# Windowed attention and a relu-squared expert: tokens brought in by casting and transposing transfers instead of by PE transposes

## The chip, the cores and the metric

The kernel runs on one core of one Trainium2 chip. The metric is the device time of one launch in microseconds (us), median of several runs. Each experiment was timed against runs of the kernel before on the same chip; a ratio is the mean time of one kernel's fast runs over that of the other's fast runs of the same rounds, so it is not quite the ratio of the medians. Chips differ: the kernel before took between 368.7 and 372.0 us (medians) on the chips used, so experiments are compared by ratio, and, where it can be done, by distances inside the traces, which mostly repeat from batch to batch to some hundredths of a us.

Engines: PE multiplies matrices (PEld loads its weights), ACT does activations, DVE elementwise work, POOL is GpSimd, SP only issues transfers. "Granted clock" is the share of PE's full clock that the records show; "half clock" is a stretch in which they show 0.5. In the kernel, SBUF is the on-chip memory that tiles live in, PSUM the one that matmuls write and other engines copy out of, and DRAM the memory off the core.

## The reference, cut to what matters

```python
# q, k, v: [8 batches, 8 heads, 576 tokens, 64]; 8 global tokens; window of 32 to each side
scores = scale * q @ k.T
mask   = (|i - j| <= 32) | is_global[i] | is_global[j]
attn   = softmax(where(mask, scores, -1e9)) @ v
x      = attn as [4608 tokens, 512]
out    = relu(x @ w_in)**2 @ w_out        # w_in [512, 2048], w_out [2048, 512]
```

Of the kernel before, what the change touches and what calls it, by code (L numbers as in the profile page):

```python
# [17 lines left out]
KT = 120  # L18
# [16 lines left out]
SCW = (456, 440)  # L35
MB = (0, 456)
NBUF = 5
# [3 lines left out]
def kernel(  # L41
# [33 lines left out]
    bufs_of = {"sc": 1, "acc": 1, "tr": 1, "mm": 3}  # L75

# [3 lines left out]
    st = {nm: sbt("st" + nm, [TP + NG, H, TJ, D], FP32) for nm in "kq"}  # L80
    st["v"] = sbt("stv", [P, NT, H, D], FP32)
    kts = [sbt(f"kt{i}", [P, NT, P], FP16) for i in range(NBUF)]
    qts = [sbt(f"qt{i}", [P, NCOL], FP16) for i in range(NBUF)]

    vts = [sbt(f"vt{i}", [P, NT, 3, D], FP16) for i in range(NBUF)]
    w_in = sbt("w_in", [P, NDM, dff], FP16)
    w_out = sbt("w_out", [P, NFF, dm], FP16)


    XOFF = 36  # L90
    xT = sbt("xT", [P, NDM, XOFF + B * S], FP16)

    nc.scalar.preload_act_table_set("natural_log_exp_and_others")


    g64 = sbt("g64", [1, NG], I64)
    src = {"k": k, "q": q, "v": v}
    gscr = {}

    def fetch_tokens(eng, nm, b, hp):  # L100
        hs = slice(2 * hp, 2 * hp + 2)
        eng.dma_start(
            out=st[nm][0:TP, hs].rearrange("p h j d -> p h (j d)"),
            in_=src[nm][b, hs].rearrange("h (p j) d -> p h (j d)", j=TJ),
        )

    def fetch_values(eng, b, hp):
        hs = slice(2 * hp, 2 * hp + 2)
        dst = st["v"]
        for h in range(2 * hp, 2 * hp + 2):  # L110
            eng.dma_start(
                out=dst[8 : 8 + KT, 0:4, h],
                in_=v[b, h, 0 : 4 * KT].rearrange("(t s) d -> s t d", s=KT),
            )
        eng.dma_start(
            out=dst[8 : 8 + KN[4], 4, hs], in_=v[b, hs, 4 * KT : S].rearrange("h s d -> s h d")
        )

    def fetch_globals(b, hp):
        def rows(nm):  # L120
            return gscr[(nm, b // 2)][b % 2, :, 2 * hp : 2 * hp + 2]


        for nm in "kq":
            js = range(TJ) if b == 2 else (TJ - 1,)
            for h in range(2):
                dst = st[nm][TP : TP + NG, 2 * hp + h, js[0] : TJ]
                nc.sync.dma_start(
                    out=dst, in_=rows(nm)[:, h].unsqueeze(1).to_broadcast((NG, len(js), D))
                )  # L130
        nc.sync.dma_start(
            out=st["v"][0:NG, :, 2 * hp : 2 * hp + 2].rearrange("p t h d -> p t (h d)"),
            in_=rows("v").rearrange("g h d -> g (h d)").unsqueeze(1).to_broadcast((NG, NT, 2 * D)),
        )

    fetch_tokens(nc.sync, "k", 0, 0)
    nc.scalar.dma_start(out=g64, in_=global_idx.unsqueeze(0))
    fetch_tokens(nc.scalar, "q", 0, 0)
    fetch_tokens(nc.scalar, "q", 0, 1)
    fetch_tokens(nc.sync, "k", 0, 1)  # L140
    fetch_values(nc.sync, 0, 0)
    fetch_values(nc.sync, 0, 1)
    fetch_tokens(nc.sync, "k", 0, 2)
    fetch_tokens(nc.sync, "q", 0, 2)
    fetch_values(nc.sync, 0, 2)
    fetch_tokens(nc.sync, "k", 0, 3)
    fetch_tokens(nc.sync, "q", 0, 3)
    fetch_values(nc.sync, 0, 3)


    idle = sbt("idle", [P, 512], FP16)
    nc.vector.memset(idle, 0.0)
    ones = sbt("ones", [1, P], FP16)
    nc.vector.memset(ones, 1.0)
    nc.scalar.copy(
        out=st["v"][0:NG].rearrange("p t h d -> p t (h d)"),
        in_=idle[0:NG].unsqueeze(1).to_broadcast((NG, NT, H * D)),
    )
# [52 lines left out]
    for kt in kts:  # L211
        nc.vector.memset(kt[:, 4, 8 + KN[4] : P], 0.0)

    def clear_values(op, vt):
        op(vt[:, :, 1], 1.0)
        op(vt[96:P, 4, 0:3:2], 0.0)

    for vt in vts[0:3]:
        clear_values(nc.gpsimd.memset, vt)


# [6 lines left out]

    gbf = sbt("gbf", [P, NG], FP32)
    g32, g32a, g32b = (sbt("g32" + x, [1, NG], I32) for x in ("", "a", "b"))  # L230
# [14 lines left out]
    def columns():  # L245
        nc.vector.tensor_scalar(out=g32a, in0=g32, scalar1=HS, scalar2=None, op0=ALU.min)
        nc.vector.tensor_scalar(
            out=g32b, in0=g32, scalar1=-255, scalar2=0, op0=ALU.add, op1=ALU.max
        )
# [15 lines left out]
    def mask_natural():  # L265
        for half in range(2):
# [17 lines left out]
    def mask_globals_matmul():  # L284


        mg = pst("acc", [P, 2, 512])
        for half in range(2):
            wins = [x for x in WIN[half] if x[3] > 8]
            for i, (t, so, c0, w) in enumerate(wins):  # L290
                o = c0 - half * BANKC
                nc.tensor.matmul(
                    mg[0:NG, half, o : o + w], oh[:, t, :],
                    mask[:, MB[half] + so : MB[half] + so + w],
                    start=(i == 0), stop=(i == len(wins) - 1), skip_group_check=True,
                )
        return mg

    far = sbt("far", [P, SCW[0] + SCW[1]], FP16)

    def mask_globals(mg, half):
        for t, so, c0, w in WIN[half]:
            for grp in range(4):
                lo, hi = max(grp * GRP, c0), min(grp * GRP + GTOK, c0 + w)
                lo, hi = max(lo, KT * t + 8 * grp), min(hi, KT * (t + 1) + 8 * grp)
                if lo < hi:
# [3 lines left out]
                        out=mask[0:NG, o : o + hi - lo], in_=mg[0:NG, half, a : a + hi - lo],  # L310
# [51 lines left out]
    def gather_rows(c):  # L362
        gsts = {nm: sbt("gst" + nm, [P, D], FP32) for nm in "kqv"}
        for nm, gst in gsts.items():
            nc.gpsimd.indirect_dma_start(
                out=gst, out_offset=None,
# [3 lines left out]
        return gsts  # L370

    def gather_store(c, gsts):
        for nm, gst in gsts.items():
            scr = dram.tile([P, D], FP32, name=f"gscr_{nm}{c}")
            nc.gpsimd.dma_start(out=scr, in_=gst)
            gscr[(nm, c)] = scr.rearrange("(b g h) d -> b g h d", b=2, h=H)



    nats = {}  # L380

    def cast_tokens(op, nm, i):
        b, hp = divmod(i, NHP)
        n = TP + NG if b > 1 else TP
        nat = nats[(nm, i)] = sbt("nat" + nm, [TP + NG, TJ, P], FP16, bufs=2)
        op(  # L386
            out=nat[0:n].rearrange("p j (h d) -> p h j d", d=D),
            in_=st[nm][0:n, 2 * hp : 2 * hp + 2],
        )

    def cast_values(op, i):
        hs = slice(2 * (i % NHP), 2 * (i % NHP) + 2)
        for tsl, n in ((slice(0, 4), P), (slice(4, 5), 8 + KN[4])):
            op(out=vts[i % NBUF][0:n, tsl, 0:3:2], in_=st["v"][0:n, tsl, hs])

    def v_globals(i):
        vs = vts[i % NBUF][:, :, 0:3:2]
# [4 lines left out]
        (nc.vector.tensor_copy if i == NHP - 1 else nc.scalar.copy)(out=gvs, in_=gl)  # L402
        nc.vector.tensor_copy(
# [4 lines left out]
    def transposed(nm, i):  # L408

        nat = nats.pop((nm, i))  # L410
        b = i // NHP
        tr = pst("mm" if b == 0 or (nm == "q" and i <= 2 * NHP) else "tr", [P, 1024], FP16)
        for j in range(TJ):
            n = TP + NG if (b > 1 and j == TJ - 1) else TP
            nc.tensor.transpose(  # L415
                tr[:, TP * j : TP * j + n], nat[0:n, j, :], identity[0:n, 0:n]
            )
        gl = tr[:, S : S + NG]
        if b < 2:
            gl = tr.bitcast(FP32)[:, 384 : 384 + NG]  # L420
            for j in range(TJ):
                nc.tensor.matmul(
                    gl, nat[0:TP, j, :], ohp[0:TP, j, :], start=(j == 0), stop=(j == TJ - 1),
                    skip_group_check=True,
                )
        return tr[:, 0:S].rearrange("p (j q) -> p q j", j=TJ), gl

    def tr_k(i, tail=None):
        tk, gl = transposed("k", i)
        kt = kts[i % NBUF]  # L430
        nc.vector.tensor_copy(
# [3 lines left out]
        (tail or nc.vector.tensor_copy)(  # L435
            out=kt[:, 4, 8 : 8 + KN[4]].rearrange("p (q j) -> p q j", j=TJ), in_=tk[:, 80:96]
        )
        nc.vector.tensor_copy(
            out=kt[:, :, 0:NG], in_=gl.unsqueeze(1).to_broadcast((P, NT, NG))
        )  # L440

    def tr_q(i, op=None):
        op = op or nc.vector.tensor_copy
        tq, gl = transposed("q", i)
        q4 = qts[i % NBUF].rearrange("p (g x) -> p g x", x=GRP)
# [5 lines left out]

# [62 lines left out]
    fills = []  # L514
    for half in range(2):
        for u in range(0, NFF, 2):
            fills.append((8 * half + 8, 2, mm1_half, (u, half)))
    for m in range(TC // P):
        for part in range(4):
            fills.append((16, 2, mm2, (0, m, part)))  # L520
    for c in range(1, NCH):
        n = (TC * (c + 1) + S - 1) // S
        ready = 16 * n + (0 if n == 2 else 4)
        for u in range(NFF):
            fills.append((ready, 2, mm1, (c, u)))
        for m in range(TC // P):
            for part in range(4):
                fills.append((ready, 2, mm2, (c, m, part)))

    def take(n):  # L530
        for _ in range(n):
            _, _, fn, a = fills.pop(0)
            fn(*a)

    credit = [0.0]

    def fill(step, n):
        credit[0] += n
        while fills and fills[0][0] <= step and credit[0] >= fills[0][1]:
# [335 lines left out]
```

## The kernel before: the parts that the change and the argument touch

Heads are handled in pairs, so a batch has four pairs; a pair is done in two halves of 288 tokens. The expert is cut into nine chunks of 512 tokens, and a chunk into 32 *units* of four matmuls with 512 columns: 16 units with the first matrix (`mm1`, each with a relu on ACT and a square on DVE) and 16 with the second (`mm2`). Units stand between the pieces of attention so that PE has work while ACT and DVE do the softmax.

```python
def cast_tokens(op, nm, i):              # f32 staging -> f16, on DVE (keys) or ACT (queries)
    ...
    op(out=nat[0:n].rearrange(...), in_=st[nm][0:n, 2 * hp : 2 * hp + 2])

def transposed(nm, i):                   # 6 PE transposes for one pair's keys or queries
    ...
    for j in range(TJ):
        nc.tensor.transpose(tr[:, TP * j : TP * j + n], nat[0:n, j, :], identity[0:n, 0:n])

def tr_k(i, tail=None):                  # three copies out of PSUM on DVE; tr_q has two more
    ...

def mm1(c, u):
    for t in range(NDM):
        nc.tensor.matmul(ph, w_in[:, t, u * P : (u + 1) * P], xT[:, t, ...], ...)
    nc.scalar.activation(out=rl, in_=ph, func=AF.Relu)
    nc.vector.tensor_tensor(out=gts[c][:, u, :], in0=rl, in1=rl, op=ALU.mult)

for i in range(2 * NHP, B * NHP):        # batches 2 to 7
    ...
    for half in range(2):
        et = scores(i, half)             # 10 matmuls in the first half, 6 in the second
        if i + 1 < B * NHP:
            (tr_k, tr_q)[half](i + 1)    # transposes for the next pair
        fill(2 * step, nf)               # two expert units
        if prev is not None:
            pv(*prev)                    # outputs of the half before
        fill(2 * step + 1, nf)           # two expert units
        casts(i + 2, half)               # casts for the pair after the next
```

After a batch's last pair, POOL writes the rows of the global tokens into `xT` (`scatter`). The first-matrix units of the chunk that follows need them.

The softmax here doesn't subtract the row's maximum and nothing guards it: scores larger than these inputs give would overflow.

## Time and profile before

| | before |
|---|---|
| time, median | 371.34 us |
| profiled span | 368.4 us |
| a steady batch (4 to 6) | 36.89 us |
| of this, 32 expert units | 27.7 us |
| first unit of chunk 1 starts | 84.19 us |
| expert work after the last attention | from 302.3 us to the end |

The page gives busy time and share of the span for each engine; the second group shows, in 40 equal slices, the busy tenths of PE, the granted PE clock and the share of the DMA engines.

```profile
PE 347.7 (94%) x2941; PEld 186.0 (51%) x2941; DVE 250.5 (68%) x656; ACT 249.2 (68%) x482; POOL 51.3 (14%) x143
PE   7779799988899999999999999999999989999995
...
PEclk9978999998999999999999999999999999999999
DMA  8999999787843663375336533652020011002002
```

Windows view, three stages: up to the first unit of chunk 1; batches 2 to 7; the rest. Columns: stretch, length, busy us of PE, PEld, DVE, ACT and POOL (instructions), granted clock, DMA share, GB/s.

```profile
0.00:84.20 84.20, 71.64 (x890) 46.55 (x891) 50.77 (x168) 50.52 (x97) 28.08 (x83) 0.96 0.95 191
84.20:302.40 218.20, 213.88 (x1765) 111.53 (x1765) 178.23 (x445) 178.37 (x350) 21.57 (x52) 0.99 0.43 114
302.40:368.00 65.60, 62.21 (x289) 27.97 (x286) 21.53 (x45) 20.36 (x35) 1.62 (x8) 1.00 0.12 45
```

PE timeline of one pair of batch 4: start, duration, what. Durations overlap: in the tail the record of a 512-column matmul lasts 379 ns, but the next one starts after 216.

```profile
153.55 0.40 PE L564 MATMUL sc<-qt_74,kt_69 64*128 64x160 f16 x10
153.88 0.43 PE L415 MATMUL tr<-identity,natk 96*128 96x96 f16 x6
154.16 1.89 PE L502 MATMUL mm<-w_out,gt 128*128 128x512 f16 x8
155.88 0.54 PE L602 MATMUL acc<-et,vt_78 128*128 128x112 f16 x6
156.26 1.89 PE L502 MATMUL mm<-w_out,gt 128*128 128x512 f16 x8
158.09 0.36 PE L564 MATMUL sc<-qt_74,kt_69 64*128 64x112 f16 x6
158.38 0.43 PE L415 MATMUL tr<-identity,natq 96*128 96x96 f16 x6
158.66 1.89 PE L502 MATMUL mm<-w_out,gt 128*128 128x512 f16 x8
160.38 0.63 PE L602 MATMUL acc<-et,vt_79 128*128 128x160 f16 x10
160.87 1.89 PE L502 MATMUL mm<-w_out,gt 128*128 128x512 f16 x8
162.69 0.39 PE L564 MATMUL sc<-qt_75,kt_70 64*128 64x160 f16 x10
```

The pair takes 162.69 - 153.55 = 9.14 us without a gap. Its eight units cost 6.92 us: in the tail the chain of waits shows 64 matmuls in 13.81 us, 0.216 us each, so 0.865 us a unit. That leaves 2.2 us of attention on PE.

### The profile page before, as it was taken

How to read it: one execution, taken by the hardware profiler on the slowest of the kernel's cores; microseconds unless marked ns; L12 is line 12 of the kernel's file. 1: busy time of each engine (PE TensorE's matmuls, PEld its weight loads, DVE VectorE, ACT ScalarE, POOL GpSimd, SP SyncE). 2: the span in 40 equal slices, each digit the busy share in tenths (PEclk: the TensorE clock that was granted, in tenths of full speed). 3: DMA queues.
4: the chain of work that ended last, by engine and by line, in shares of the span. 5: the costliest groups of instructions: out<-in, count | busy, mean ns of one | idle time of the engine just before them, and what ended most of it. 6: DMA issues, size and time to landing. Idle time of an engine off the chain costs nothing.

```text
span 368.4 us, 8258 instructions
## 1 busy us (share of the span) xinstructions
PE 347.7 (94%) x2941; PEld 186.0 (51%) x2941; DVE 250.5 (68%) x656; ACT 249.2 (68%) x482; POOL 51.3 (14%) x143
## 2 busy tenths in 40 slices
PE   7779799988899999999999999999999989999995
PEld 3556575544445555555555555555555544444442
DVE  7753566656888878977897789778977953422421
ACT  6656574465997799679967996799679942612610
POOL 5364430016000610020002000200020001000000
PEclk9978999998999999999999999999999999999999
DMA  8999999787843663375336533652020011002002
GB/s 196 192 147 201 193 228 201 188 188 193 188 130 97 188 166 94 90 188 142 95 93 187 142 95 93 187 140 60 30 87 2 0 52 64 0 30 85 0 32 85
DMA packets 65011, 43.93 MB, mean 119 GB/s; under 512 B 42730, under 2 KB 60074, under 8 KB 64970
## 3 DMA queue, kind: packets, MB, share of 16 engines
q1 hardware_dynamic: 59752, 38.03, 40.0%
q0 software_dynamic: 4800, 4.79, 7.9%
q10 hardware_dynamic: 418, 0.59, 0.7%
q8 instruction: 23, 0.38, 0.5%
q14 instruction: 18, 0.15, 0.1%
HBM read 37.85 MB, written 9.73 MB: 129 GB/s over the span
## 4 chain that ended last, share of the span: by engine, by line
PE 60%; issue 14%; DVE 7%; DMA 6%; ACT 5%; POOL 4%; POOLq 2%; ACTq 0%; SPq 0%; DVEq 0%
PE mm L502 25%; PE mm L460 24%; PE acc L602 4%; PE tr L415 3%; DMA w_in<-in_moe_w_in_dram 3%; PE sc L564 3%; DVE gt L466 2%; DMA stq<-in_q_dram 2%; POOLq L649 2%; ACT rl L465 2%; DMA stv<-in_v_dram 1%; POOL xT L658 1%; ACT er L570 1%; ACT natq L386 1%; DVE et L574 1%
## 5 line engine op out<-in xcount | busy, mean ns | idle before, releaser
L502 PE MATMUL mm<-w_out,gt 128*128 128x512 f16 x576 | 133.6, 379 | 0.0
L460 PE MATMUL mm<-xT,w_in 128*128 128x512 f16 x512 | 120.7, 382 | 1.0 <-POOL xT L658 1.0
L465 ACT ACTIVATE rl<-mm 128x512 f16<-128x512 f32 x128 | 72.2, 595 | 34.6 <-PE mm L460 33.9
L502 PEld LDWEIGHTS <-gt 128*128 128x128 f16 x576 | 53.1, 97 | 55.6
L460 PEld LDWEIGHTS <-w_in 128*128 128x128 f16 x512 | 47.7, 98 | 51.2 <-issue 2.9
L612 ACT ACTIVATE rec<-acc 64x288 f32<-64x288 f32 (+1 forms) x112 | 45.5, 406 | 33.9 <-PE acc L602 24.1
L638 DVE TENSOR_TENSOR xT<-acc,rec 64x288 f16<-64x288 f32 (+1 forms) x112 | 50.9, 454 | 19.8 <-ACT rec L613 18.0
L466 DVE TENSOR_TENSOR gt<-rl 128x512 f16<-128x512 f16 x128 | 50.2, 421 | 18.2 <-ACT rl L465 17.5
L658 POOL COPY xT<-gx 128x4 f16 (+2 forms) x80 | 21.8, 272 | 231.1 <-DVE xT L638 226.8
L570 ACT ACTIVATE er<-sc 128x912 f16<-128x912 f32 (+1 forms) x48 | 44.0, 917 | 5.4 <-PE sc L564 5.0
L574 DVE TENSOR_TENSOR et<-er,mask 128x912 f16<-128x912 f16 (+1 forms) x48 | 29.9, 623 | 21.2 <-ACT er L570 20.9
L508 DVE COPY ot<-mm 128x512 f32<-128x512 f32 x36 | 24.9, 691 | 26.0 <-PE mm L502 25.3
L613 ACT ACTIVATE rec<-rec 128x288 f32<-128x288 f32 x64 | 28.3, 443 | 2.0
L386 ACT CAST natq<-stq 104x768 f16<-104x768 f32 (+1 forms) x32 | 26.4, 824 | 4.4 <-DMA stq<-in_q_dram 4.4
L570 ACT ACTIVATE et<-sc 128x912 f16<-128x912 f32 (+1 forms) x16 | 14.6, 915 | 12.0 <-PE sc L564 11.7
L386 DVE CAST natk<-stk 104x768 f16<-104x768 f32 (+1 forms) x32 | 17.7, 552 | 0.3
L479 PE MATMUL mm<-xT,w_in 128*128 128x256 f16 x128 | 16.8, 290 | 0.6 <-POOL xT L658 0.6
L479 PEld LDWEIGHTS <-w_in 128*128 128x128 f16 x128 | 12.7, 104 | 3.3 <-issue 0.6
L617 DVE TENSOR_REDUCE gs<-acc 128x16 f32<-128x32 f32 x32 | 6.0, 187 | 12.2 <-ACT rec L612 12.2
L415 PE MATMUL tr<-identity,natk 96*128 96x96 f16 x168 | 12.1, 208 | 1.9 <-DVE natk L386 1.8
L415 PEld LDWEIGHTS <-natq 96*128 96x128 f16 x192 | 9.2, 98 | 7.1 <-ACT natq L386 1.5
L491 DVE TENSOR_TENSOR gt<-rl 128x512 f16<-128x512 f16 x16 | 6.8, 426 | 8.4 <-ACT rl L490 8.1
(205 smaller groups left out, 324.2 us busy)
## 6 DMA issues: line engine op xcount, KB each, us to landing
stk<-in_k_dram SPq DMA_DIRECT2D x32, 288.0 KB
out_dram<-ot SPq DMA_DIRECT2D x36, 256.0 KB
stq<-in_q_dram SPq DMA_DIRECT2D x30, 288.0 KB
stv<-in_v_dram SPq DMA_DIRECT2D x64, 120.0 KB
w_in<-in_moe_w_in_dram POOLq DMA_DIRECT2D x4, 512.0 KB, 9.5
w_out<-in_moe_w_out_dram POOLq DMA_DIRECT2D x4, 512.0 KB, 9.0
stv<-in_v_dram SPq DMA_DIRECT2D x32, 48.0 KB
stq<-in_q_dram ACTq DMA_DIRECT2D x2, 288.0 KB
```

Source lines behind the costliest of these rows:

```text
L386: op(out=nat[0:n].rearrange("p j (h d) -> p h j d", d=D), in_=st[nm][0:n, 2 * hp : 2 * hp + 2],)
L415: nc.tensor.transpose(tr[:, TP * j : TP * j + n], nat[0:n, j, :], identity[0:n, 0:n])
L460: nc.tensor.matmul(ph, w_in[:, t, u * P : (u + 1) * P], xT[:, t, XOFF + c * TC : XOFF + (c + 1) * TC], start=(t == 0), stop=(t == NDM - 1),)
L465: nc.scalar.activation(out=rl, in_=ph, func=AF.Relu)
L466: nc.vector.tensor_tensor(out=gts[c][:, u, :], in0=rl, in1=rl, op=ALU.mult)
L479: nc.tensor.matmul(ph[:, j], w_in[:, t, (u + j) * P : (u + j + 1) * P], xT[:, t, half * (256 + XOFF) : half * (256 + XOFF) + 256], start=( ...
L502: nc.tensor.matmul(po, gts[c][:, f, m * P : (m + 1) * P], w_out[:, f, :], start=(f == 0), stop=(f == NFF - 1),)
L570: nc.scalar.activation(out=er[:, :, 0:W], in_=sc[:, :, 0:W], func=AF.Exp, bias=0.0, scale=scale)
L574: nc.vector.tensor_tensor(out=et[:, :, 0:W], in0=er[:, :, 0:W], in1=mask[:, MB[half] : MB[half] + W].unsqueeze(1).to_broadcast((P, 2, W)), ...
L612: nc.scalar.activation(out=rec[r], in_=av[rs, xs, :, 0:GTOK], func=AF.Ln)
L613: nc.scalar.activation(out=rec, in_=rec, func=AF.Exp, scale=-1.0)
L638: nc.vector.tensor_tensor(out=xT[r, hp, x0 : x0 + HS].rearrange("p (k x) -> p k x", k=2), in0=av[r, x, :, 0:GTOK], in1=rec[r], op=ALU.mult,)
```

## The change

Intent: take token preparation off PE, DVE and ACT. For batches 2 to 7, POOL issues transfers that cast f32 to f16 on the way. Keys and queries go into a scratch in DRAM, from which SP fetches them with two transposing transfers per batch. Values are cast straight into SBUF. The rows of global tokens reach the scratch by few transfers. The windows of the first half that are 8 columns wide go (`WIN2`); the sums over global columns are added from both halves instead. A pair becomes one block (`unit` in the code, not to be taken for an expert unit): both halves' scores, then both outputs, with expert units between (2, 1 and 4 of them, more in a batch's last pairs). Batch 0 keeps PE transposes, batch 1 gets casting loads and PE transposes. The first gather of global rows is issued ahead of the second expert matrix.

```diff
+    def tokens_to_scratch(b):
+        for nm in "kq":
+            n, step, pitch, off = {"k": (NT, KT, P, NG), "q": (4, GTOK, GRP, 0)}[nm]
+            for x in range(n):
+                lo, hi = x * step, min((x + 1) * step, S)
+                pool.dma_start(
+                    out=scr[(nm, b % 2)][...].rearrange("s (h d) -> s h d", d=D),
+                    in_=src[nm][b, :, lo:hi].rearrange("h s d -> s h d"),
+                )
+    def transposes(b):
+        for nm, d_, w in (("k", kb, KW), ("q", qb, QW)):
             ...
+            nc.sync.dma_start_transpose(out=d_[b], in_=scr[(nm, b % 2)][:, :])
...
+    def unit(i, n, nxt=None):
+        scs = [scores(i, half, pair_tag[half], WIN2) for half in range(2)]
+        et = [weights(half, scs[half], WIN2) for half in range(2)]
+        take(n[0])
         ...                                   # batch 1 only: PE transposes of the next pair
+        for half in range(2):
+            acc = outputs(i, half, et[half], pair_tag[half], WIN2)
+            finish_outputs(i, half, acc)
+            if half == 0:
+                take(n[1])
+        if i % NHP == NHP - 1:
+            scatter(i // NHP)
+        take(n[2])
+    for hp in range(NHP):
+        unit(NHP + hp, (1, 1, 2) if hp < NHP - 1 else (1, 1, 2), ...)   # batch 1
+    take(99)
+    for b in range(2, B):
+        queue += units[b + 1]
+        for hp in range(NHP):
+            unit(NHP * b + hp, ((2, 1, 4), (2, 1, 4), (2, 1, 5), (2, 1, 7))[hp])
+            if hp == 0 and b + 1 < B:
+                if b > 2 and b % 2:
+                    gather((b + 1) // 2)
+                globals_to_scratch(b + 1)
+                tokens_to_scratch(b + 1)
+                transposes(b + 1)
                 ...
+                values(b + 1)
+                value_globals(b + 1)
+        take(99)
```

## The prediction

> **What bounds the kernel now.** By the windows view PE is busy 35.7 of 36 us in a steady batch (197 to 233 us); ACT 30.4, DVE 29.7, mean DMA share 0.46. One batch takes 36.9 us (the chain of waits repeats at 152, 189, 226, 262 us). In the chain's tail 64 expert matmuls take 13.81 us, 216 ns each, so one 512-token chunk (128 matmuls) is 27.6 us of the 36.9; the other 9.2 us is attention on PE: scores, outputs and transposes. Batches 0 and 1 end at about 84 us, with DMA at 0.8 to 1.1 of its engines (weights plus three batches of tokens) and only some 30 of 288 expert units done. After attention ends (302 us) 62 us are expert matmuls back to back. Fixed: 249 us of expert matmuls.
>
> **Removed.** For batches 2 to 7: 48 PE transposes per batch (12 per pair, about 0.9 us a pair in the timeline), their PSUM copies on DVE (0.65+0.25+0.17 us for keys, 0.76 for queries), casts on DVE (0.55 us) and ACT (0.82 for queries, 0.8 for values), and the 8-column windows (8 matmuls a pair). A pair's scores and outputs then stream 3520 columns; at 0.42 ns each (216/512) that is 1.5 us, with overhead 1.6 to 1.9 us, against 2.3 now. Estimate: a PE-bound batch of 34 to 35 us. Batch 1 also loses its mask-adding matmuls.
>
> **Added.** Each batch's q and k go through DRAM: nine casting transfers into scratch, two DMA transposes; values come by five casting transfers. All casts are issued by POOL: 13,800 pieces of 256 bytes a batch. The existing casting load (512 pieces) holds POOL 0.75 to 0.9 us, so I estimate 1.3 us for some 1000 pieces, 18 us of POOL per batch, beside 2.9 us of scatter. The 256-byte value loads of before take 18 to 32 ns on a DMA engine. At 20 ns the pieces cost 17 us of 16 engines per batch; with transposes and stores about 26 us: it fits in 35. The Trainium skill (DMA: Bandwidth & Descriptors, Specifications) puts line rate at 512 bytes or more and warns of read-modify-write below; the casts write 128-byte runs. No trace here shows what such a DRAM write costs. At 40 ns the sum would be about 38 us and DMA would become the limit.
>
> **Critical path.** The next batch's tokens are issued after the first pair (7.5 us into the batch) and needed at its end, so 26 us are there for issue (12), landing (2.5) and transposes (5 to 8): I expect it to fit with some us to spare. Relus, exps and logarithms in the first two pairs ask ACT for 8.6 us where PE needs 7.5: up to 1 us lost a batch.
>
> **Sum.** Batch 1 ends near 82 us (DMA-bound like now: weights 26 us of engine time, tokens of three batches); 6 x 35 = 210; a tail of two chunks, 55, plus 4 for ends: 351 us of span, 3 more as timed.
>
> **Predicted 353 us, range 341 to 378; faster by over 2% 0.75, within 2% 0.12, slower 0.13.**
>
> **What would show it.** Right: PE over 90% in every batch, batch period 34 to 35 us, no transposes on PE after batch 1, ACT and DVE near 60%, mean DMA share near 0.8, key and query transposes landing before the last units of each batch. Wrong: PE gaps at the start of each batch's scores, released by the DMA of the key or query tile; 256-byte casting pieces over 35 ns; POOL's transfers issued late; batch 1 ending after 90 us.
>
> **What would make it wrong.** Slow 128-byte DRAM writes, or slow descriptor making on POOL: each us of lateness costs six us. Faster, if batches 0 and 1 shrink well below 80 us.

## The result, and the profile after

The changed kernel takes 354.94 us (median; 354.48 to 356.61) against 371.34: ratio 0.9557, 95% interval 0.952 to 0.9594. Faster by 4.4%. The predicted time was 353.

```profile
PE 323.2 (92%) x2305; PEld 167.5 (47%) x2305; DVE 218.8 (62%) x548; ACT 217.7 (62%) x434; POOL 125.9 (36%) x211
PE   6878599684899999999999999999999999999995
...
PEclk9989879988799999999999999999999999999999
DMA  8999999921999169949992999499810011011011
```

PE, DVE and ACT each lost 24 to 32 us of busy time, POOL gained 75. The DMA digits hide that the share goes over 1: the records of small packets overlap. The slices with low PE (the fifth, eighth and tenth, of 8.8 us each) lie before 90 us.

The three stages by the windows view (columns as above):

```profile
0.00:89.40 89.40, 66.40 (x718) 42.50 (x719) 57.36 (x168) 52.36 (x116) 47.49 (x87) 0.91 1.21 152
89.40:293.60 204.20, 201.55 (x1333) 100.14 (x1333) 141.57 (x339) 146.19 (x286) 78.40 (x124) 0.99 1.08 109
293.60:352.80 59.20, 55.27 (x257) 24.85 (x254) 19.83 (x41) 19.11 (x32) 0.00 (x0) 1.00 0.11 41
```

In both traces chunk 0 is complete when chunk 1 begins, so the first stage holds the same expert work: it became 5.2 us *longer*. In the other two stages the same 256 units are shared out differently (64 instead of 72 are left for the tail); together they fell from 284.2 to 263.4 us, by 20.8. The sum is the measured 15.6 us of span.

PE timeline of batch 3's third pair, and the head of its fourth:

```profile
139.93 0.36 PE L583 MATMUL sc<-qb,kb 64*128 64x160 f16 x6
140.13 0.35 PE L583 MATMUL acc<-qb,kb 64*128 64x112 f16 x6
140.42 1.90 PE L487 MATMUL mm<-xT,w_in 128*128 128x512 f16 x8
142.16 0.55 PE L625 MATMUL sc<-et,vb 128*128 128x160 f16 x6
142.54 1.03 PE L529 MATMUL mm<-w_out,gt 128*128 128x512 f16 x4
143.40 0.55 PE L625 MATMUL acc<-et,vb 128*128 128x112 f16 x6
143.78 4.48 PE L529 MATMUL mm<-w_out,gt 128*128 128x512 f16 x20
148.20 0.36 PE L583 MATMUL sc<-qb,kb 64*128 64x160 f16 x6
```

Third pair: 148.20 - 139.93 = 8.27 us with eight units (6.92), so 1.35 us of attention. The fourth pair is alike: 9.99 us with ten units, 1.34. The first two pairs, which carry seven first-matrix units each, take 7.70 and 7.88 us, that is 1.64 and 1.83 over their units. Batches 3 to 6 take 33.84 us each, and no PE wait of over 0.3 us is listed in them. (Batch 2 takes 40.8 us; its extra 7 us lie in its first pair, with the waits shown next.)

The early stage does have waits. PE timeline from batch 1's last outputs past the first units of chunk 1; in brackets the idle time and what ended it:

```profile
80.82 1.03 PE L529 MATMUL mm<-w_out,gt 128*128 128x512 f16 x4
81.68 0.55 PE L625 MATMUL acc<-et,vb 128*128 128x112 f16 x6
83.53 0.37 PE L583 MATMUL sc<-qb,kb 64*128 64x160 f16 x6 [1.30 <-DVE xT L676]
86.61 0.55 PE L583 MATMUL acc<-qb,kb 64*128 64x112 f16 x6 [2.72 <-DVE xT L676]
89.38 3.57 PE L487 MATMUL mm<-xT,w_in 128*128 128x512 f16 x8 [2.23 <-POOL xT L695]
92.75 0.66 PE L625 MATMUL sc<-et,vb 128*128 128x160 f16 x6
```

PE first waits for PSUM tiles that the outputs before have to leave (DVE `xT`), then for POOL's scatter. The eight matmuls at 89.38 take 92.75 - 89.38 = 3.37 us, 421 ns each instead of 216. The Trainium skill (TensorE: Matmul & The Clock Gate, What's actually happening) says that an idle window of about 3.4 us halves PE's clock and a busy one restores it. This trace agrees on the length: its clock record holds half clock in stretches of 3.4 or 6.8 us, four of them before 93 us, 20.5 us in all, against 10.2 us in three stretches of before. But PE need not be idle for a whole window: in the 3.41 us before each of the four stretches it was still busy for 1.68, 0.42, 1.50 and 0.37 us.

POOL's queue at the head of batch 4 (the scatter of batch 3, then the transfers of batch 5):

```profile
155.92 2.06 POOL L695 COPY xT<-gx 128x4 f16 x8 [14.91 <-DVE xT L676]
158.33 4.35 POOL L389 DMA_DIRECT2D scr_k<-in_k_dram  x5 [0.35 <-issue]
162.17 4.17 POOL L389 DMA_DIRECT2D scr_q<-in_q_dram  x4
165.73 5.01 POOL L113 DMA_DIRECT2D vb<-in_v_dram  x5
```

Fourteen transfers hold POOL from 158.33 to 170.74, 12.4 us; the durations add up to more, because records of single transfers overlap here too. They go out at 158.3, when PE begins the first scores of batch 4 (158.19), not after its first pair as the prediction read the source: POOL waits for nothing that the first pair makes. In the trace's packet records the last transposing packets of each batch end 6 to 16 us before the scores that read them.

### The profile page after: what moved, and what is told of

Same layout as the page of the kernel before. It is cut to its first block, busy times and chain, and to the rows that moved or that the text cites. A ratio compares the mean times of both kernels' runs of the same rounds, so it can differ in the third digit from the quotient of the medians.

```text
span 352.8 us, 6563 instructions
## 1 busy us (share of the span) xinstructions
PE 323.2 (92%) x2305; PEld 167.5 (47%) x2305; DVE 218.8 (62%) x548; ACT 217.7 (62%) x434; POOL 125.9 (36%) x211
## 4 chain that ended last, share of the span: by engine, by line
PE 58%; ACT 13%; issue 12%; DMA 6%; POOL 5%; DVE 4%; another core or an unknown queue 0%; POOLq 0%; ACTq 0%
PE mm L529 32%; PE mm L487 17%; ACT rl L492 6%; DMA w_out<-in_moe_w_out_dram 4%; ACT et L592 4%; POOL vb L113 3%; PE mm L506 3%; ACT rec L648 2%; DMA vb<-in_v_dram 2%; DVE xT L676 2%; PE sc L625 2%; PE sc L583 1%; PE acc L625 1%; DVE gt L493 1%; ACT rec L649 1%
## 5 line engine op out<-in xcount | busy, mean ns | idle before, releaser
L487 PEld LDWEIGHTS <-w_in 128*128 128x128 f16 x512 | 47.8, 98 | 60.9 <-issue 10.2
L592 ACT ACTIVATE et<-sc 128x880 f16<-128x880 f32 (+1 forms) x32 | 29.0, 905 | 44.1 <-PE sc L583 38.9
L596 DVE TENSOR_TENSOR et<-et,mask 128x880 f16<-128x880 f16 x60 | 37.0, 617 | 29.4 <-ACT et L592 29.0
L113 POOL DMA_DIRECT2D vb<-in_v_dram x40 | 42.2, 1686 | 1.5 <-DMA w_out<-in_moe_w_out_dram 0.9
L676 DVE TENSOR_TENSOR xT<-sc,rec 64x288 f16<-64x288 f32 (+1 forms) x62 | 28.2, 455 | 10.4 <-ACT rec L649 8.4
L625 PEld LDWEIGHTS <-vb 128*128 128x128 f16 x360 | 26.9, 99 | 14.0 <-issue 1.3
L592 ACT ACTIVATE et<-acc 128x880 f16<-128x880 f32 (+1 forms) x32 | 29.1, 908 | 5.6 <-PE acc L583 4.5
L676 DVE TENSOR_TENSOR xT<-acc,rec 64x288 f16<-64x288 f32 (+1 forms) x62 | 28.2, 455 | 5.4 <-ACT rec L649 4.8
L648 ACT ACTIVATE rec<-sc 64x288 f32<-64x288 f32 (+1 forms) x62 | 25.1, 404 | 7.9 <-PE sc L625 6.5
L389 POOL DMA_DIRECT2D scr_k<-in_k_dram x30 | 26.5, 1120 | 1.2 <-issue 1.2
L389 POOL DMA_DIRECT2D scr_q<-in_q_dram x24 | 25.4, 1699 | 0.0
```

What stands on the lines that cost most here:

```text
L113: pool.dma_start(out=vb[b][NG - back : NG + KN[x], x, 2 * hs.start : 2 * hs.stop : 2], in_=v[b, hs, x * KT - back : x * KT + KN[x]].rearra ...
L389: pool.dma_start(out=scr[(nm, b % 2)][x * pitch + off : x * pitch + off + hi - lo].rearrange("s (h d) -> s h d", d=D), in_=src[nm][b, :, l ...
L592: act.activation(out=et[:, :, 0:W], in_=sc[:, :, 0:W], func=AF.Exp, bias=0.0, scale=scale)
L596: dve.tensor_tensor(out=et[:, :, 0:W], in0=et[:, :, 0:W], in1=mask[:, MB[half] : MB[half] + W].unsqueeze(1).to_broadcast((P, 2, W)), op=AL ...
L625: nc.tensor.matmul(acc[:, e, o : o + w], vtf[:, t, vo : vo + P], et[:, e, so : so + w], start=(n == 0), stop=(n == nw - 1), skip_group_che ...
L648: act.activation(out=rec[r], in_=av[rs, xs, :, 0:GTOK], func=AF.Ln)
```

## The experiments

All results were correct, and all runs fast except one of e10. "Changed" stands for the changed kernel, ratio 0.956. The theory: batches 2 to 7 are faster because PE has fewer instructions to stream and ACT and DVE had been relieved far enough not to take over; the first stage became slower because batch 1 has too few units between its pairs. Rivals: the gain is the relief of ACT and DVE alone; DMA sets the period; the first stage is bound by DMA.

### e1: the PE transposes put back as dead work

```diff
+    def extra_pe(i):
+        if i < 2 * NHP:
+            return
+        w = pst("tr", [P, 1024], FP16)
+        for j in range(TJ):
+            nc.tensor.transpose(w[:, TP * j : TP * j + TP], idle[0:TP, 0:P], identity[0:TP, 0:TP])
...
         take(n[0])
+        extra_pe(i)
...
                 take(n[1])
+                extra_pe(i)
```

> The changed kernel with 12 PE transposes of 96x128 put back into every pair of batches 2 to 7, on zeros and read by nobody. In the kernel before, six such transposes stand 0.27 to 0.28 us apart, start to start. Theory A (PE's stream of matmuls alone sets the period of 33.84 us): +0.55 us a pair, 24 pairs, +13 us, period about 36.1 us. Theory B (the gain came from relieving ACT and DVE of casts and copies): at most +3 us, because ACT and DVE are untouched.

Measured 362.37 us, ratio 0.981 (0.9749 to 0.9871). The trace is clearer. PE timeline of e1 in the third pair of a batch, one of the two added groups and what follows it:

```profile
143.78 0.42 PE L820 MATMUL tr<-identity,idle 96*128 96x96 f16 x6
144.04 0.55 PE L625 MATMUL sc<-et,vb 128*128 128x160 f16 x6
```

Six transposes again cost 0.26 us. The third and fourth pair became 8.78 and 10.51 us, 0.51 and 0.52 longer: PE's stream sets them. But the first two became 7.92 and 7.92, only 0.22 and 0.04 longer: something else had already been setting those. The period rose by 1.3 us, not 2.2. So theory A holds for half of the batch only, and the total fell short of the expected 13 us.

### e2 and e3: work put back on ACT, on DVE

The two edits are drawn together here; both act in batches 2 to 7 only.

```diff
+    d32 = sbt("d32", [P, 768], FP32)          # zeros
+    d16 = sbt("d16", [P, 768], FP16)
...
         take(n[0])
+        act.copy(out=d16[:, 0:768], in_=d32[:, 0:768])           # e2, batches 2 to 7
+        dve.tensor_copy(out=d16, in_=d32)                        # e3 instead
+        dve.tensor_copy(out=d16[:, 0:512], in_=wp[0])            # e3: out of PSUM
```

> The changed kernel with one ACT cast of 128x768 from f32 (0.82 us, the query cast that the change took away) in every pair of batches 2 to 7, on zeros. ACT goes from about 27 to 30 us of a 33.8 us batch, its share of before. Theory A (PE alone): +0 to 2 us. Theory B (ACT and DVE relief): the whole 0.82 us a pair, +15 to 20 us. Between them, if ACT is full only in the pairs that carry first-matrix units: +0.8 us in two pairs a batch, +8 to 10 us.

> The changed kernel with one DVE cast of 128x768 and one DVE copy of 128x512 out of PSUM (about 0.55 + 0.69 us) in every pair of batches 2 to 7. DVE goes from about 25 to 30 us a batch, its share of before. Theory A (PE alone): +0 to 2 us. Theory B: 1.2 us a pair, up to +28 us.

e2: 362.36 us, ratio 0.9808 (0.9747 to 0.987). e3: 354.43 us, ratio 0.9596 (0.9537 to 0.9655), which cannot be told from the changed kernel. In e3's trace batch 3's pairs take 7.70, 7.89, 8.30 and 9.99 us, as without the load; in some batches the third takes up to 0.3 us more, so that the mean period is 34.0 us. In e2's they take 8.40, 8.59, 8.26 and 9.99. Most of the ACT work, 0.70 us of a cast whose record lasts 0.85, shows in each of the first two pairs, and nothing in the others. There PE waits for relus (PE timeline of e2, first pair):

```profile
129.68 2.81 PE L487 MATMUL mm<-xT,w_in 128*128 128x512 f16 x12
133.27 1.02 PE L487 MATMUL mm<-xT,w_in 128*128 128x512 f16 x4 [0.78 <-ACT rl L492]
```

Together, e1 to e3 settle the period: the two pairs with seven relus are set by ACT, the other two by PE, DVE sets almost nothing. The rival "relief of ACT and DVE alone" falls, and so does "PE alone". In the changed kernel's own trace ACT works through the first pair of batch 3 without an idle stretch, from the first exp at 124.75 us to the next pair's at 132.65. ACT's relief was needed to reach the gain. Had the query cast stayed on ACT, 1.4 us of the 3.05 would be lost again.

### e4: the 8-column windows put back

```diff
-        scs = [scores(i, half, pair_tag[half], WIN2) for half in range(2)]
+        scs = [scores(i, half, pair_tag[half], (WIN[0], WIN2[1])) for half in range(2)]
         # the same for weights and outputs; global sums from the first half alone
```

> The changed kernel with the two 8-column windows of the first half back in all 28 pairs after batch 0 (8 more matmuls a pair; the sums over global columns are then taken from the first half alone, result unchanged). In the trace of before ten score matmuls take 0.32 us and six 0.29, ten output matmuls 0.49 and six 0.39, so Theory A: +0.13 us a pair, +3 us or about +1%. If the windows were the larger part of the gain (rival): +8 us or more.

Measured 356.95 us, ratio 0.967 (0.9612 to 0.9728). Batch 3's pairs: 7.77, 7.92, 8.42 and 10.14, so 0.15 us where PE sets the pair. The period rose by 0.41 us. The windows are the smaller part, as expected; the total is about 1 us above what was expected, within the intervals.

Of the 0.87 us that a PE-set pair lost against before (2.21 to 1.34), the transposes are 0.52 and the windows 0.15. The last 0.2 us was not tried: the order of the pieces, and the fewer changes from one kind to another, changed together. Before, the last pair of a batch took 0.3 us more than the others, a wait of its transposes for DVE's copy of keys (0.27 us at 186.14 us); it is gone as well.

### e5, e6 and e10: the next batch's transfers later

e5 and e6 move the block of transfers in the source.

```diff
-            if hp == 0 and b + 1 < B:
+            if hp == 1 and b + 1 < B:          # e5; hp == 2 in e6
```

> The changed kernel with the next batch's transfers (gather, casts into scratch, transposes, values) issued after the second pair instead of after the first, about 7.5 us later. The last transposing packets of the changed kernel end 6 to 11 us before the scores that read them. Theory S (the DMA chain has that slack and no more): +0 to 2 us for each of five batches, +0 to 8 us in all. Rival (DMA share near 1 means DMA already sets the period): +7.5 us for each batch, +37 us.

> The same, issued after the third pair, about 15 to 16 us later than in the changed kernel. Theory S: the lateness minus the slack, 15.5 minus 6 to 11, so 4.5 to 9.5 us for each of five batches, +25 to +45 us, with PE gaps at the head of each batch. If DMA had been the limit: +75 us.

e5: 354.05 us, ratio 0.9563. e6: 358.07 us, ratio 0.9678 (0.9638 to 0.9719). Both expectations rested on a mistake. In the traces the casting packets start when they did before (127.0 and 160.1 us in e5, 126.8 and 159.9 in changed), because POOL runs ahead of PE, and its own order, scatter then transfers, is the same. Only SP's queue was reordered: in e6 its transposing transfers stand behind output stores that wait for expert results, and PE waits four times for keys and queries, 3.0 us in all, and three times for the values of global tokens, 0.8 us. The longest:

```profile
160.30 0.37 PE L583 MATMUL sc<-qb,kb 64*128 64x160 f16 x6 [1.78 <-DMA qb<-scr_q]
```

So e5 and e6 say nothing about later casting. e10 makes POOL wait by a true dependence:

```diff
-            if hp == 0 and b + 1 < B:
+            if hp == 1 and b + 1 < B:
+                x0 = XOFF + b * S + HS
+                pool.tensor_copy(out=gate, in_=xT[0:1, 1, x0 : x0 + 1])
```

> e5 and e6 did not move the casting transfers: the trace shows them starting at the same time, because POOL runs ahead and issues them right after its scatter. Here one tiny POOL copy that reads an output of the second pair stands ahead of the next batch's transfers, so that they start about 11.5 us later than in the changed kernel (138.5 instead of 127 us in batch 3). Theory S (the transfers have 7 to 13 us of slack before the next batch's first scores, and DMA does not set the period): lateness 0 + 4.7 + 0.8 + 5.5 + 2.7 us in the five batches, +8 to +16 us in all, PE waiting for the key or query tile. Rival (transfers set the pace): 11.5 us for each batch, +50 us or more. No slack to speak of and no loss would be under +3 us.

e10: 402.72 us, ratio 1.0797 (1.0727 to 1.0868; one of its four runs was slow and is left out). Far above what theory S gave, and near the "+50 us or more" of the rival, so the total alone does not decide. Its largest entry in the waits view of PE from 80 us on (total, times, longest), and then one of these waits in the PE timeline:

```profile
PE sc L583 <- DMA qb<-scr_q: 33.3, 5, 9.5
```

```profile
171.78 0.55 PE L583 MATMUL sc<-qb,kb 64*128 64x160 f16 x6 [8.38 <-DMA qb<-scr_q]
```

Two terms had been mis-sized. POOL's first packets of a batch's transfers left 15.5 to 19 us later, counted from the batch's first scores, than in changed, and not 11.5. The pair that POOL waited for itself ends later when the batch begins at half clock. And after every wait PE ran at half clock: the clock record holds five such stretches at the batch heads, of 6.8 to 13.7 us, where changed has none after 93 us. The waits average 33.3 / 5 = 6.7 us, so some 11 us of each delay were absorbed; had the transfers no slack, the five delays (87 us in all) would all show as waits. This agrees with the 6 to 16 us seen in the packet records: DMA does not set the period of the changed kernel, but a transfer that is later than its slack is paid for with PE's clock as well. How the 14 us beyond the waits (the span grew by 47 us, the waits are 33) divide between clock and refilling the pipeline was not separated.

### e7: batch 1's units spread

```diff
-    take(6)
     clear_ones(dve.memset, vb[1])
     take(1)
     tr_k(NHP, tag="tr")
     take(1)
     tr_q(NHP, tag="mm", op=act.copy)
-    take(2)
...
-        unit(NHP + hp, (1, 1, 2) if hp < NHP - 1 else (1, 1, 2), ...)
+        unit(NHP + hp, (1, 1, 3) if hp < NHP - 1 else (1, 1, 5), ...)
```

> The changed kernel with chunk 0's 24 waiting expert units moved: 2 instead of 10 before batch 1, 5 instead of 4 in each of its first three pairs, 7 in the last. No transfer is touched. Theory F (batch 1 ends late because its pairs have too few expert units to cover the wait for a free PSUM tile, 11 us of PE waits between 42 and 92 us): first chunk-1 matmul at 80 to 83 us instead of 89.4, total -6 to -9 us. Rival (that stretch is bound by DMA): no gain, or a wait for the value or key tiles of batch 1 in place of the old one.

Measured 347.36 us, ratio 0.9397 (0.9359 to 0.9435): 1.6 points below changed, about 6 us, clear of both intervals. In the trace the first unit of chunk 1 starts at 83.40 us instead of 89.38, and the period stays at 33.84. The head of that stretch, to be read against the same place above:

```profile
77.45 4.48 PE L529 MATMUL mm<-w_out,gt 128*128 128x512 f16 x20
81.86 0.37 PE L583 MATMUL sc<-qb,kb 64*128 64x160 f16 x6
82.07 0.35 PE L583 MATMUL acc<-qb,kb 64*128 64x112 f16 x6
83.40 1.89 PE L487 MATMUL mm<-xT,w_in 128*128 128x512 f16 x8 [0.98 <-POOL xT L695]
```

The two waits for PSUM are gone, the wait for the scatter is 1 us, and the units of chunk 1 run at full clock. No transfer was touched. So the loss of the first stage was a matter of where the units stand, and not of DMA.

### e8: only the clock kept

```diff
+    keep_warm(16)                       # 16 matmuls on zeros
     queue += units[1] + units[2]
...
     take(99)
+    keep_warm(16)
     for b in range(2, B):
```

> The changed kernel with 16 matmuls on zeros ahead of the second half of chunk 0 and 16 more between batch 1 and batch 2, where PE waits for the scatter (3.8 us and 5 us). The clock record shows half clock from 41.8 to 48.6 us and 86.2 to 93 us. If that half clock costs what it takes from the busy part of these stretches (about 6 + 3.6 us at half speed): -3 to -5 us. If the stretch is bound by what the scatter releases and not by PE's speed: within 1 us.

Measured 352.75 us, ratio 0.9539 (0.9509 to 0.9569): the interval overlaps that of changed (0.952 to 0.9594), so a gain is not shown. The half clock from 42 to 49 us did go (the windows view gives a granted clock of 1.00 there), and the first unit of chunk 1 stood at 86.00 us. But that unit again ran at half clock, 3.36 us for eight matmuls, and behind the added matmuls PE still waited 0.6 us for PSUM and 2.5 for the scatter. The half clock follows the waits. What curing it alone is worth stays open: only the first of the two stretches was cured, and the profiled span is 2.4 us shorter.

### e9: the first gather behind the second matrix

```diff
     gather_index()
-    gather(0)
     for j in range(4):
         pool.dma_start(out=w_out[:, ts(j, 4), :], in_=wo[:, ts(j, 4), :])
+    gather(0)
```

> The changed kernel with the first gather (rows of the global tokens of batches 0 and 1) issued after the four transfers of the second expert matrix instead of ahead of them; one part of the change undone. In the changed kernel POOL issues the gathers from 14.6 to 18.3 us, then waits for first-matrix transfers to complete (1.7 and 1.8 us) before the last two transfers of the second matrix, and starts the scatter at 26.8 us. If the place of the gathers matters only through POOL's queue: the scatter starts some 2 us later, batch 1's rows land later but before 51 us where they are read, total +0 to +3 us against the changed kernel (ratio 0.956 to 0.964). If batch 1 then waits for its global rows behind the second matrix's bytes: +4 us or more, with PE or SP waits for the gathered rows ahead of batch 1's transposes.

Measured 356.35 us, ratio 0.9642 (0.9569 to 0.9714). The interval overlaps that of changed: the ratios differ by some 3 us, and that this part of the change is worth anything is not shown. The trace shows the path: the gathers, and the loads behind them, wait for earlier transfers in POOL's queue, the second scatter begins at 42.44 us instead of 40.13, and the first unit of chunk 1 at 90.50 instead of 89.38. No wait for the gathered rows appears.

### f1 and f2: further versions

f1 is e7 with the scatter of batch 0's second half moved ahead of value transfers in POOL's queue, and 12 matmuls on zeros in that gap. f2 is f1 with four second-matrix units of each chunk held back for the next batch.

```diff
     globals_to_scratch(2)
-    for x in range(2):
-        fetch_values(1, x)
...
     scatter(0, 1)
-    for x in range(2, NT):
+    keep_warm(12)
+    for x in range(NT):
         fetch_values(1, x)
...                                          # f2 only:
-        queue += units[b + 1]
+        first, second = units[b + 1][:NFF], units[b + 1][NFF:]
+        queue += first[:5] + held + first[5:] + second[:-4]
+        held = second[-4:]
```

> e7 (units spread over batch 1), plus the scatter of batch 0's second half moved ahead of two value transfers for which POOL was waiting on other transfers' completion, plus 12 matmuls on zeros in that gap to keep the clock. e7 still waits 4.1 us there and runs 42.5 to 52.8 us at half clock. If both are real costs: first chunk-1 matmul at 78 to 80 us instead of 83.4, total 342 to 345 us, ratio 0.926 to 0.933. If the value tiles of batch 1 or the tokens of batch 2 come too late: no gain against e7 (0.940), with PE waits for these tiles.

> f1 with the last four second-matrix units of each chunk held back and put among the first-matrix units of the next batch, so that the first two pairs of batches 3 to 7 carry 5 relus instead of 7. e1 and e2 showed these two pairs to be set by ACT (1.64 and 1.83 us over their expert units, against 1.34 in the pairs without relus). Theory: the period falls from 33.84 to about 33.05 us, 5 batches, -3 to -4 us against f1, ratio 0.917 to 0.924. If the excess of these pairs is something else (PSUM, first-matrix matmuls themselves): no change of period.

f1: 346.13 us, ratio 0.9313 (0.9265 to 0.9362). f2: 347.19 us, ratio 0.932 (0.9266 to 0.9374). Both beat both kernels; their intervals touch e7's, so more than e7 is not shown. In f1's trace the wait for the scatter fell from 4.1 to 1.2 us, but outputs then waited 1.3 us for a value tile. f2's first two pairs take 7.40 us, 1.34 over their seven units: with five relus PE sets them, as the theory says. But the third pair, now with six relus, rose from 8.27 to 8.76, so that the period fell by 0.3 us and not 0.8. The relus were moved rather than spread.

## Why the prediction was right, and where not

The time (354.9 against 353) and the direction were right, and so was the mechanism of batches 2 to 7. That the time came within 2 us was luck: two misses cancel. Predicted: 82 + 210 + 59 = 351 us of span. Measured: 89.4 + 204.2 + 59.2 = 352.8.

- **PE-bound batches, right; the size off.** "A PE-bound batch of 34 to 35 us", entered as 35, measured 33.84, and the stage 204.2 against 210. The mis-sized term is "scores and outputs ... 1.6 to 1.9 us" a pair, which measured 1.34 where PE sets the pair. The estimate streamed 3520 columns one after another. But six score matmuls of 880 columns cost 140.13 - 139.93 = 0.20 us, and the next six 0.29, where six output matmuls of 880 columns cost 0.38: the two heads' scores use 64 rows each, start 4 ns apart and run side by side. The Trainium skill says that such row tiles work in parallel (TensorEngine Tiling, Key Properties); the trace agrees, and the trace of before would have shown it.
- **Transposes, mis-sized.** "About 0.9 us a pair in the timeline" added durations (0.43 twice). Start to start it is 0.56, and e1 measured 0.52. The error did not enter the sum.
- **ACT in the first two pairs, right.** "Up to 1 us lost a batch"; the excess of the two pairs is 0.30 + 0.49 = 0.8 us, and e2 shows that ACT is the cause. The "8.6 us" that it gave ACT for such a pair measured 7.9.
- **DMA fits, right; its terms off.** A casting piece was put at 20 ns on an engine; its record lasts 32 ns. But records overlap: when casts for scratch ran without transposes, each of the 16 engines took one piece per 15 to 19 ns, so the stated limit ("At 40 ns ... DMA would become the limit") was drawn from the wrong quantity. POOL's 18 us of issue measured 12.4: the 1.3 us for "some 1000 pieces" assumed a cost that grows with the pieces, but a transfer of 1152 pieces took 0.77 us from start to start, where one of 512 took 0.75 to 0.86.
- **Issue after the first pair, wrong.** "The next batch's tokens are issued after the first pair ... so 26 us are there". POOL runs ahead and issues right after the scatter; from the first casting packet to the scores that need the tokens there are about 31 us. It cost nothing in the sum, but e5 and e6 were built on it.
- **Batch 1 "near 82 us (DMA-bound like now)", wrong.** It measured 89.4. From 68 to 84 us the DMA share was 0.01 to 0.27, so DMA is not what bound it there. PE had 11 us of waits between 42 and 92 us for PSUM tiles and scatters, because the pairs of batch 1 carry four units each where those of the other batches carry seven or more, and ten had been spent before. e7 won 6 us back with no transfer changed. The sign named for it ("batch 1 ending after 90 us") came close, for another cause.

## What to carry to other kernels

Read what an instruction whose record overlaps the next one costs from start-to-start distances, pair by pair: they showed here that half of a batch was set by PE and half by ACT, which whole-kernel averages of 92% and 62% hide. When filler work is finite, give it to the places where the engine would wait, including the seams between stages; spreading the same units was worth a third again of the whole change. And before moving an instruction in the source, check which engine's queue it is in and what that queue really waits for.

## What the Trainium skill lacked or had wrong

- *DMA: Bandwidth & Descriptors*, Specifications: under 512 bytes it warns of read-modify-write, and says nothing of its size. Casting pieces that write 128 bytes lasted 32 ns each whether they wrote DRAM or SBUF; no extra cost of DRAM was seen. At one piece of 256 bytes read per 15 to 19 ns and engine, that is some 220 to 270 GB/s read.
- The same page, Anatomy of one DMA, calls descriptor generation "small, variable" and gives no time for a transfer. Here a casting transfer held POOL, from start to start, 0.66 to 0.68 us for 384 pieces, 0.69 to 0.81 for 768 or 960 (keys), 0.77 to 0.79 for 1152 (queries) and 0.89 to 0.92 for 960 written into SBUF (values).
- The same page, Latency and other measured facts, gives 261 GB/s for a transposing transfer with a non-contiguous middle dimension and about 350 to 400 for the contiguous case. Here two transfers from a scratch that is read row by row, 1.28 MB together, took 6.0 to 6.4 us when no casts ran beside them (e6), 199 to 212 GB/s, and 11 to 14 us beside casts.
- *Perfetto Trace Analysis* tells in its part on HWDGE transfers that the issuing queue is held until the descriptors are made, but not for how long. A transposing transfer held SP's queue for 4.1 to 8.4 us beside casts, and for 2.6 to 3.2 us without them (e6).
- *TensorE: Matmul & The Clock Gate* tells one matmul's latency from the gap to the next, but not that the profile's duration of a *group* hides the same difference: six transposes read 0.43 us and cost 0.28.
- The same page does not say how idle a window must be for PE's clock to be halved; here 1.68 us of work in 3.41 did not prevent it.
- *Perfetto Trace Analysis* (Identifying the Most-Contended Engine) warns against DMA occupancy, but not that a share made of packet records can exceed 1 (2.2 in the stretch from 48 to 52 us), so that a share near 1 is no sign of a limit.
